# Sums as single steps, a narrower U-product, a first pair in two halves and a new order, in a fused attention and low-rank mixer kernel

## The chip, the cores and the metric

The kernel runs on one NeuronCore of a Trainium2 chip. A core has five engines with instruction queues of their own: TensorE (PE) for matmuls, VectorE (DVE), ScalarE (ACT) and GpSimd (POOL) for elementwise work, and SyncE (SP), which here only issues DMAs. POOL issues most of the loads through a DMA queue of its own, SP the first loads, the transposes by DMA and the stores. Every engine works through its own list in order; semaphores make one wait for another. The metric is the time of one execution on the device in microseconds (us), lower is better.

## The reference

The inputs are q, k, v of 4 batches x 8 heads x 768 tokens x 64, U (768 x 32), V (32 x 768), w_ch1 (512 x 2048) and w_ch2 (2048 x 512), all float32.

```python
scores = scale * np.matmul(q, k.transpose(0, 1, 3, 2))
keep = is_global | is_local          # 8 global keys, 96 local ones, causal
scores = scores + bias[None, :, :, :]            # -slope(head) * distance
scores = np.where(keep, scores, -1000000000.0)
a = np.exp(scores - max); a = a / a.sum()
x = np.matmul(a, v)                  # 4 x 768 x 512, heads side by side
h = x^T @ U @ V                      # rank 32, over the tokens
u = x + h^T
out = u + np.maximum(u @ w_ch1, 0.0) @ w_ch2
```

So: a banded attention, a token mixer of rank 32 with a residual, and an MLP of 512 to 2048 to 512 with a residual.

## The kernel before, in words

The work is cut into 16 pairs of heads (batch b = pair // 4) and, for each batch, an MLP. Every piece of work is a `Task` with a name, an engine and what it depends on (lines 100 to 130). The tasks are put out in an order that is written out by hand, the string `ORDER` (line 23 and on): `Planner.run` (line 135) only checks it against the dependencies and the buffers, and takes the buffer numbers from `SLOTS`. So each engine's list is the order's own, cut to that engine. Attention of the next batch is woven into the MLP of the batch before it.

The names, with p the pair, b the batch:

- `lkp`, `lqp`, `lvp`: loads of K, Q, V (`add_load`, line 345). Pair 0's K and Q come as float32 by SP into scratch memory, and `Ck0.h`, `Cq0.h` cast them to half precision, one head each. All other loads are cast by the DMA, on POOL's queue. `w1_i` and `w2_i` load the weights.
- `TKp`, `TQp`: K and Q are turned, so that the head dimension lies on the partitions (`arrange`, line 531): six 128x128 matmuls with an identity for pairs 0 and 4 to 7, twelve of half width for pairs 1 to 3, a DMA transpose for pairs 8 to 15. `EKp`, `EQp` copy the result from PSUM; pair 0's copy is split in two halves of the tokens. `KOp` is K with the 32 first keys put in front of each block.
- `SBp.s`, `Sp.s`, `EXp.s`, `MKp.s`: bias by matmul (batch 0 alone), scores, exp on ACT, and a multiplication by the mask on DVE (batches 1 to 3). `PVp`: probabilities times V, with a column of ones for the sums; `VCp`, `VGp` prepare V. `RCp`, `NMp`: the division, into `x_sb`; `XCp`: x in half precision.
- `UPp` (`mixed`, line 754): x @ U. For pairs 0 to 7 it also turns x into uT by six identity matmuls (L759); for pairs 8 to 15 `XTp` does that by DMA. The U part (L764) is six 128x128 matmuls per pair whose weights are `uz` (U four times over, so that its 32 columns fill 128) and whose moving operand is x. `TEp` copies the result to `tmp`, `HMp` multiplies it by V, `E0p` and `E1p` bring it to uT.
- MLP-1: u @ w_ch1. Batch 0 does it directly but for one unit (`M1a` to `M1d`, L927 and L951, relus `RL`, `RM`). All else is done by seven products for a 2x2 block of output instead of eight (`ZP1b.z` to `ZP7b.z`, L1024; z is a unit, 0 to 7). They need sums of blocks of w_ch1, `ZSz` (line 998, four DVE instructions of 256 columns for a unit, kept over the batches), and sums of blocks of u, `ZTb` (line 977, four DVE instructions of 768 columns in one task). `ZU`, `ZW`, `ZX` copy partial sums on ACT, `ZA`, `ZB`, `ZD` add and clip on DVE (L1042), `ZR` is a relu on ACT.
- MLP-2, in the same manner: `PAb.g`, `PBb.g` form sums of the hidden layer on DVE (two instructions each, lines 1091 to 1101), `TWa`, `TWb` sums of w_ch2 (line 467), `P1b.t` to `P7b.t` are the products of eight matmuls of 256 columns (`prod`, L1141), `RSb.t` puts the mixer's part in PSUM ahead of them (L1133), `DA` to `DH` add the results to x, `Ob.t` stores.
- `w0` to `w23`: matmuls of zeros that fill PE (L1240).

PE changes between matmuls on 64 rows (`S`, `HM`, `RS` and the half-width turns) and on 128 rows (all others).

Of the kernel before, what the change touches and what calls it, by code (L numbers as in the profile page):

```python
# [21 lines left out]
lk0 ones2 ones3 vz wz iota w6 lq0 ones0 relf w1 lk1 w4 rel3 bias1 bias0 w2 lq1 w0 w3 lk3 mask3 SB0.2 Ck0.0 Ck0.1 vs1  # L22
mask1 TK0 lv0 w7 Cq0.0 EK0.1 SB0.0 w5 mask7 lk2 Cq0.1 bias2 EK0.0 TQ0 lq3 SB0.1 KO0.1 EQ0.1 ones1 EQ0.0 KO0.0 lq2
S0.2 TK1 EX0.2 lv1 S0.1 EK1 TQ1 EX0.1 S0.0 lv2 EQ1 TK3 EX0.0 SB1.0 KO1 u16 SB1.1 bias4 S1.1 VC0 EK3 S1.0 vs0 uz SB1.2
VG0 lv3 EX1.0 KO3 S1.2 TK2 EX1.2 PV0 EK2 EX1.1 lk5 TQ3 RC0 NM0 TQ2 EQ3 SB2.1 KO2 SB2.2 EQ2 SB2.0 VC1 lk4 S2.0 VG1
S2.1 XC0 EX2.0 S2.2 PV1 EX2.2 VC2 lq4 SB3.1 uc EX2.1 RC1 back S3.1 mixl NM1 SB3.2 EX3.1 S3.2 VG2 lq5 SB3.0 VC3 VG3
S3.0 mask0 TK5 EX3.0 PV2 EK5 w1_1 EX3.2 PV3.0 RC2 UP0 RC3.0 w1_7 NM2 XC1 TK4 PV3.1 w1_5 TE0 EK4 PV3.2 XC2 HM0 RC3.1
lv4 RC3.2 UP1 NH3.1 E00 NH3.0 UP2 NM3 w1_3 TE1 UP3.0 TE2 UP3.1 NH3.2 w1_2 KO4 HM1 HM2 E01 TQ5 E02 w1_4 UP3.2 TQ4 TE3
EQ5 lk6 M1a0.3 EQ4 M1c0.3 HM3 S4.1 E13 E03 M1d0.3 EX4.2 lv5 ZT0 M1a0.2 M1c0.2 M1b0.3 EX4.1 w1_0 M1a0.15 RL0.3 M1b0.14
VC4 KO5 M1a0.14 RM0.14 w1_6 vs2 RL0.15 M1d0.2 mask2 S5.0 S4.0 M1b0.2 EX4.0 M1a0.11 EX5.0 MK4.0 M1b0.7 lk7 VG4 RL0.2  # L30
M1a0.7 MK4.2 RM0.7 MK4.1 M1b0.15 RL0.14 ZS3 M1b0.10 RL0.11 mask5 M1b0.6 MK5.0 RL0.7 RM0.15 lq7 ZS7 S5.1 RM0.10
M1b0.11 EX5.2 ZS6 PV4 w2_3 EX5.1 M1a0.10 lq6 RM0.11 M1b0.8 MK5.1 RM0.6 M1a0.8 RC4 RL0.10 NM4 VC5 ZP10.5 w2_1 ZP20.5
RM0.8 ZS5 M1a0.6 ZU0.5 RL0.8 M1a0.1 MK5.2 w2_2 mask6 TK6 M1c0.1 RL0.6 EK6 w2_0 ZP60.5 M1d0.1 TD0 ZW0.5 PA0.3 M1b0.1
lv6 VG5 M1b0.12 PA0.1 ZP50.5 RM0.12 M1b0.4 RL0.1 TK7 ZA0.5 RM0.4 ZP70.5 lq8 PB0.1 PV5 mask4 KO6 M1a0.5 EK7 ZX0.5 RC5
M1a0.4 lk9 NM5 RL0.5 TQ6 RL0.4 TQ7 ZB0.5 KO7 M1a0.12 EQ6 XC5 M1a0.0 EQ7 M1c0.0 lv8 PB0.3 ZP40.5 XC4 ZP30.5 M1d0.0
RL0.12 ZD0.5 M1b0.0 ZR0.5 M1b0.5 RL0.0 PA0.2 S7.0 lv7 RM0.5 UP4 EX7.0 PA0.0 S6.1 TE4 RS0.1 EX6.2 HM4 PB0.2 P20.1 E04
PB0.0 UP5 EX6.1 P10.1 TWa1 lk8 TE5 S6.0 RS0.0 EX6.0 HM5 DA0.1 P20.0 TWa0 lv9 VC6 P30.0 E05 lq10 TWb0 P50.0 VG6 P50.1
TWb1 lq9 P30.1 DF0.0 P60.1 MK6.1 TK8 P10.0 DF0.1 lk10 ZS2 S7.1 VG9 EX7.1 RS0.2 MK6.0 P10.2 DA0.0 EX7.2 MK6.2 P20.2
TQ8 DC0.1 VC7 PV6 MK7.2 VG7 TK9 P60.0 DB0.1 MK7.0 DA0.2 P70.1 RC6 TQ9 DB0.0 MK7.1 P60.2 DD0.1 NM6 PV7 TQ10 P40.1 RC7
XC6 NM7 VC9 lq12 P30.2 DB0.2 XC7 VG8 ZS4 UP6 KO8 UP7 lv11 DG0.1 DF0.2 TE6 P70.0 TE7 ZS1 lk11 HM7 HM6 S8.0 E07 E06  # L40
P50.2 DD0.0 lv14 DC0.0 E17 ZP11.6 KO9 ZT1 ZP11.7 lk12 P70.2 ZU1.7 ZU1.6 ZP21.7 EX8.0 P40.0 lq11 ZA1.7 ZP61.7 DG0.0
S8.1 ZW1.7 MK8.0 VC11 ZP21.6 DD0.2 EX8.2 ZP71.7 ZS0 P40.2 ZX1.7 ZA1.6 EX8.1 ZP11.5 DC0.2 ZP51.7 ZP41.7 ZU1.5 DG0.2
O0.2 ZP61.6 MK8.1 ZR1.7 S9.1 O0.3 ZB1.7 EX9.1 ZP11.4 TK11 ZP61.5 ZP31.7 ZU1.4 MK9.1 ZP21.4 ZW1.5 ZP21.5 O0.1 ZD1.7
EX9.2 ZP61.4 ZP71.5 ZA1.4 ZP21.3 ZA1.5 O0.0 ZX1.5 ZP51.5 ZW1.6 ZP11.3 ZB1.5 ZP51.6 ZW1.4 TK10 ZP71.6 MK9.2 ZU1.3
ZP31.5 ZP71.4 ZA1.3 ZP51.4 ZD1.5 ZX1.4 ZP11.2 VC8 TD1 ZP41.5 ZX1.6 ZB1.4 ZP61.3 VG11 ZP21.2 ZB1.6 ZW1.3 ZP31.4 MK8.2
ZR1.5 ZP31.6 ZP41.4 ZU1.2 ZD1.4 O0.5 ZP71.3 ZR1.4 ZA1.2 ZP61.2 O0.4 ZX1.3 ZP51.3 ZD1.6 TQ12 ZW1.2 S9.0 ZB1.3 ZP11.0
EX9.0 ZP71.2 PA1.2 ZP41.3 ZU1.0 ZP41.6 TQ11 ZX1.2 ZP31.3 MK9.0 ZR1.6 ZP51.2 ZD1.3 PV8 ZR1.3 ZB1.2 TK12 ZP61.0 RC8
ZP11.1 NM8 ZP31.2 lv12 ZU1.1 ZP21.1 ZW1.0 ZP21.0 ZD1.2 XC8 ZP61.1 ZA1.1 ZP51.0 ZP41.2 ZA1.0 ZW1.1 XT8 ZP71.0 PB1.2
ZR1.2 ZP71.1 ZX1.0 UP8 ZP51.1 ZX1.1 ZB1.0 PV9 TE8 KO12 KO10 PA1.3 ZP31.0 ZP41.1 ZP41.0 ZB1.1 lv10 ZR1.1 HM8 ZD1.0
ZR1.0 ZP31.1 RC9 VC12 lk13 RS1.1 ZD1.1 P21.1 KO11 NM9 P11.1 VG12 E08 lq13 S10.1 PA1.0 RS1.0 EX10.2 P11.0 lk14 PA1.1  # L50
EX10.1 P21.0 DA1.0 XC9 S10.0 PB1.3 lq15 S11.0 P51.0 EX10.0 XT9 PB1.0 EX11.0 P51.1 lq14 PB1.1 S11.1 MK11.0 P61.0
EX11.2 DA1.1 lk15 P31.0 EX11.1 DB1.0 MK11.2 P31.1 VC10 MK11.1 UP9 DF1.0 VG10 PV11 MK10.2 TE9 VC14 P61.1 RC11 NM11
lv15 P71.0 DF1.1 XC11 HM9 S12.0 RS1.2 E09 XT11 EX12.0 P11.2 DD1.0 MK10.0 S12.1 TQ14 MK10.1 EX12.1 P21.2 DB1.1 VG14
DC1.0 PV10 TK14 DA1.2 P71.1 RC10 NM10 lv13 P61.2 DD1.1 XC10 UP11 P31.2 EX12.2 TE11 XT10 DC1.1 P41.0 MK12.1 DB1.2 HM11
DF1.2 UP10 P71.2 DG1.0 TE10 KO14 E111 P41.1 MK12.2 VC13 E011 ZP12.6 VG13 DD1.2 S14.0 DG1.1 ZU2.6 HM10 P41.2 EX14.0
E010 O1.0 ZP12.7 ZT2 O1.1 S14.1 ZU2.7 VC15 EX14.1 ZP22.7 P51.2 VG15 EX14.2 ZP22.6 MK14.0 ZP62.6 ZA2.7 ZP52.7 TK15
ZW2.6 ZP62.7 MK12.0 ZP52.6 DC1.2 ZW2.7 ZP72.6 ZP22.4 ZA2.6 ZX2.6 O1.2 ZP72.7 ZP12.4 ZB2.6 TQ15 ZX2.7 ZP42.6 DG1.2
# [106 lines left out]
def kernel(  # L164
# [180 lines left out]
    def add_load(p):  # L345
# [23 lines left out]
        def one(src, dst, g, nm, i):  # L369
            if direct(p, nm):  # L370
                i += 2 * p

                def ldf():
                    nc.sync.dma_start(*by_token(stg32[i], src))
# [527 lines left out]
    def mlp(b):  # L902
# [84 lines left out]
        for z in units:  # L987
# [5 lines left out]
            def sw(i, gs=gs, z=z, a21=a21):  # L993
                if gs is None:
                    return a21 if i == 0 else zs[ZK.index(z)][:, i - 1]
# [296 lines left out]
```

## Time and profile before

| | us |
|---|---|
| median of 3 runs (217.62 to 218.74) | 217.62 |
| the profiled execution | 217.54 |
| its span | 215.8 |
| PE busy | 211.1 |
| DVE busy | 189.3 |
| ACT busy | 138.2 |
| POOL busy | 72.2 |
| first exp starts | 8.11 |
| first MLP matmul starts | 26.85 |
| first product of MLP-2 starts | 54.21 |
| last product of MLP-2 starts | 209.72 |

The span runs from the first to the last instruction of the profiled execution; the time of the execution is 1.7 us longer. Busy means that an instruction of the engine was under way. PE's matmuls overlap, so a busy PE may still be spaced more widely than it could be: the distance from the start of one to the start of the next tells more than the length of one. Times in the text count from the start of the span. The trace gives instructions by line; the names of tasks were put to them by their place in each engine's order.

### The profile page before, as it was taken

The numbers are of one execution on the slowest core, as the hardware profiler recorded it, in microseconds if no ns is written. First come the engines' busy times: TensorE is split into PE (matmuls) and PEld (weight loads), VectorE is DVE, ScalarE is ACT, GpSimd is POOL, SyncE is SP. The second block draws the span as 40 slices with busy tenths as digits, with TensorE's granted clock in tenths as the row PEclk, the third lists the DMA queues.
The fourth block names the chain that finished last, engine by engine and source line by source line (L and its number), as shares of the span: only waits on it lengthen the run. The fifth ranks groups of instructions, "written<-read, shape, count | busy, mean of one in ns | idle before, by whom it ended". The sixth has DMA issues, their size and how long they took to land.

```text
span 215.8 us, 5747 instructions
## 1 busy us (share of the span) xinstructions
PE 211.1 (98%) x2298; PEld 153.7 (71%) x2298; DVE 189.3 (88%) x417; ACT 138.2 (64%) x255; POOL 72.2 (33%) x95
## 2 busy tenths in 40 slices
PE   8998999999999989999999999999999999999996
PEld 3565855676889866566787875667789766668896
DVE  4687977999999998999999899999999975999680
ACT  6999989989924669789886467785722068730000
POOL 8989967873670860013961100000000000000000
DMA  6999999999999999779999957651002310000543
GB/s 166 175 168 156 145 180 177 181 194 196 154 151 157 147 156 159 179 185 127 141 132 129 121 155 144 185 94 36 3 0 51 74 49 3 2 2 3 219 149 122
DMA packets 100731, 26.78 MB, mean 124 GB/s; under 512 B 87744, under 2 KB 98112, under 8 KB 100704
## 3 DMA queue, kind: packets, MB, share of 16 engines
q0 software_dynamic: 71312, 13.34, 80.1%
q1 hardware_dynamic: 29392, 13.07, 28.3%
q8 instruction: 18, 0.29, 0.6%
q14 instruction: 9, 0.07, 0.1%
HBM read 27.56 MB, written 6.29 MB: 157 GB/s over the span
## 4 chain that ended last, share of the span: by engine, by line
PE 91%; ACT 5%; DVE 2%; issue 1%; POOL 0%; POOLq 0%
PE ps L1141 35%; PE ps L1024 26%; PE ps L927 6%; PE ps L652 4%; ACT ep L717 4%; PE ps L1240 3%; PE ps L951 3%; PE ps L764 3%; PE ps L781 2%; PE ps L780 2%; PE ps L521 2%; PE ps L871 2%; PE ps L759 1%; PE ps L1133 1%; PE ps L633 1%
## 5 line engine op out<-in xcount | busy, mean ns | idle before, releaser
L717 ACT ACTIVATE ep<-ps 128x1024 f16<-128x1024 f32 (+1 forms) x48 | 43.9, 957 | 13.3 <-PE ps L652 12.5
L1141 PEld LDWEIGHTS <-htr 128*128 128x128 f16 x392 | 36.3, 98 | 7.3 <-issue 2.3
L265 ACT ACTIVATE zu<-ps 128x384 f32<-128x384 f32 x59 | 27.5, 491 | 8.5 <-PE ps L1024 7.6
L1042 DVE CUSTOM_DVE_ANT_0 htr<-ps,zu 128x384 f16<-128x384 f32 x59 | 31.0, 551 | 1.0 <-PE ps L1024 0.4
L1153 DVE TENSOR_TENSOR x_sb<-x_sb,ps 128x256 f32<-128x256 f32 (+1 forms) x60 | 27.1, 463 | 3.6 <-PE ps L1141 3.1
L1141 PEld LDWEIGHTS <-sA 128*128 128x128 f16 x288 | 27.5, 98 | 3.6
L364 POOL DMA_DIRECT2D vt<-in_v_dram x16 | 16.5, 1032 | 31.7 <-PE ps L781 22.4
L1024 PEld LDWEIGHTS <-w 128*128 128x128 f16 x200 | 18.9, 98 | 11.3 <-issue 0.2
L1141 PE MATMUL ps<-tB,htr 128*128 128x256 f16 (+1 forms) x200 | 24.0, 268 | 0.0
L1141 PE MATMUL ps<-w,sA 128*128 128x256 f16 x192 | 23.6, 273 | 0.0
L1141 PE MATMUL ps<-w,htr 128*128 128x256 f16 x192 | 23.5, 273 | 0.0
L360 POOL DMA_DIRECT2D stgq<-in_q_dram x24 | 19.9, 854 | 10.1 <-DMA qT<-stgq 7.2
L1024 PE MATMUL ps<-uT,w 128*128 128x384 f16 x100 | 23.0, 326 | 0.0
L1024 PE MATMUL ps<-zt,w 128*128 128x384 f16 x100 | 22.6, 326 | 0.0
L360 POOL DMA_DIRECT2D stgk<-in_k_dram x24 | 20.4, 872 | 4.1 <-DMA w<-in_moe_w_ch_dram 2.5
L265 ACT ACTIVATE x<-x_sb 128x768 f16<-128x768 f32 x13 | 10.9, 845 | 10.4 <-DVE x_sb L819 10.3
L730 DVE TENSOR_TENSOR ep<-ep,mask 128x1024 f16<-128x1024 f16 x24 | 16.3, 684 | 0.5 <-ACT ep L717 0.5
L819 DVE TENSOR_TENSOR x_sb<-ps,rcp 128x768 f32<-128x768 f32 x16 | 15.2, 952 | 0.3
L1024 PE MATMUL ps<-zt,zs 128*128 128x384 f16 x64 | 15.3, 326 | 0.0
L927 PE MATMUL ps<-uT,w 128*128 128x384 f16 x80 | 14.7, 326 | 0.0
L652 PE MATMUL ps<-qT,kT 64*128 64x128 f16 x192 | 14.1, 217 | 0.0
L652 PE MATMUL ps<-qT,kO 64*128 64x128 f16 x160 | 12.8, 218 | 1.0 <-DVE htr L1042 0.7
(119 smaller groups left out, 408.6 us busy)
## 6 DMA issues: line engine op xcount, KB each, us to landing
out_dram<-x_sb SPq DMA_DIRECT2D x20, 256.0 KB, 2.4
vt<-in_v_dram POOLq DMA_DIRECT2D x16, 192.0 KB, 7.0
stgk<-in_k_dram POOLq DMA_DIRECT2D x24, 96.0 KB, 6.0
stgq<-in_q_dram POOLq DMA_DIRECT2D x24, 96.0 KB, 5.6
w<-in_moe_w_ch_dram POOLq DMA_DIRECT2D x8, 256.0 KB, 8.6
w<-in_moe_w_ch_dram POOLq DMA_DIRECT2D x4, 512.0 KB, 9.8
out_dram<-x_sb SPq DMA_DIRECT2D x7, 128.0 KB, 2.2
vo<-vt SPq DMA_DIRECT2D x5, 123.8 KB, 2.5
```

The costliest lines, as they stand in the source:

```text
L265: nc.scalar.activation(dst, src, AF.Copy)
L360: nc.gpsimd.dma_start(o[:, i], src[b, h0 + i].rearrange("(n p) d -> p n d", p=P))
L364: nc.gpsimd.dma_start(vt[gv.slot][:, :, :, 0:D], v[b, h0:h0 + 2].rearrange("h (n p) d -> p h n d", p=P),)
L652: nc.tensor.matmul(t[:, hi, j * P:(j + 1) * P], lhs, qt[r, i * P:(i + 1) * P], start=not biased, stop=True, skip_group_check=biased,)
L717: nc.scalar.activation(ep[gep.slot][:, :, lo:512], ps[:, gsc.slot:gsc.slot + 2, lo:512], AF.Exp, scale=qk_scale)
L730: nc.vector.tensor_tensor(ev, ev, mv, ALU.mult)
L819: nc.vector.tensor_tensor(xo, pvo()[:, :, :, 0:D], rcp[p % 2].unsqueeze(3).broadcast_to((P, 2, NB, D)), ALU.mult)
L927: nc.tensor.matmul(ps[:, g.slot, 0:HS], w1[:, dc, jt * P:(jt + 1) * P], ub[:, dc, i * HS:(i + 1) * HS], start=(dc == 0), stop=(dc == NDC - 1),
L1024: nc.tensor.matmul(bank(g), a()[:, i], bq[:, i], start=first and i == 0, stop=last and i == 1, skip_group_check=True,)
L1042: return lambda: nc.vector._custom_dve(TENSOR_ADD_SAT, out=o, in0=x(), in1=y(), s0=3.0e38, s1=0.0)
L1141: nc.tensor.matmul(o if part is None else o[:, part], a[:, j, c0 + cols.start:c0 + cols.stop], bq[:, j] if part is None else bq[:, j, part ...
L1153: nc.vector.tensor_tensor(o, o, x, ALU.add)
```

## The change

Five things are changed at once.

1. The sums of w_ch1 are formed for two units at a time (`ZYay` to `ZYdy`, y = unit // 2): four instructions of 512 columns for two units instead of eight of 256. Each instruction is a task of its own.
2. So are the instructions of `ZT` (`ZTa` to `ZTd`), of the sums of w_ch2 (`TWa` to `TWd`) and of the hidden layer (`PA`, `PB`, `PC`, `PD`). What needs one of these sums now waits for that one, not for all.
3. In pairs 4 to 15 the U part has x as weights and 32 columns of `uz` as the moving operand. Its result stands the other way round, so `XEp` (ACT) copies it to `tmp`, four times over, `XUp` turns it by one 128x128 matmul, and `TEp` copies that.
4. Pair 0's K and Q are loaded in two halves of 64 partitions (four DMAs on SP), cast in four pieces each and turned in two sets of six 64-row matmuls, each with its own PSUM bank.
5. `ORDER`, `SLOTS` and some choices of engine are new. From ACT to DVE go EK3, EQ5, KO4, KO6, KO9, KO10, TE4, TE8, TE9 and XC7; from DVE to ACT KO1, KO15, E01, EQ7, TE11, TE15 and XC15; from SP to ACT KO12, KO13 and the V copies of pair 8; from ACT to SP KO14 and the V copies of pairs 12 and 14. Pair 0's casts and copies are dealt out anew between ACT and DVE.

```diff
-lk0 ones2 ones3 vz wz iota w6 lq0 ones0 relf w1 lk1 w4 rel3 bias1 bias0 w2 lq1 w0 w3 lk3 mask3 SB0.2 Ck0.0 Ck0.1 vs1
+lq0.0 wz iota vz w5 lk0.0 w6 relf lq1 w0 lk0.1 rel3 bias0 bias1 w3 lk1 lq0.1 bias2 w4 bias4 ones0 w1 lk3 w7 Ck0.1 lv0
...
+KO0.0 TQ0.1 uz lq3 KO0.1 EQ0.1 TQ1 lq2 S0.0 EQ1 S0.2 EX0.0 lv1 TK1 S0.1 EX0.2 EK1 SB1.0 u16 TK3 KO1 SB1.2 ones2 EK3
...
-RL0.12 ZD0.5 M1b0.0 ZR0.5 M1b0.5 RL0.0 PA0.2 S7.0 lv7 RM0.5 UP4 EX7.0 PA0.0 S6.1 TE4 RS0.1 EX6.2 HM4 PB0.2 P20.1 E04
-PB0.0 UP5 EX6.1 P10.1 TWa1 lk8 TE5 S6.0 RS0.0 EX6.0 HM5 DA0.1 P20.0 TWa0 lv9 VC6 P30.0 E05 lq10 TWb0 P50.0 VG6 P50.1
+ZP40.5 ZD0.5 UP4 RL0.0 PD0.1 M1b0.5 XE4 PA0.2 ZR0.5 S7.0 PD0.3 RM0.5 XU4 EX7.0 TE4 S6.1 PA0.0 HM4 EX6.1 PC0.2 RS0.0
+P10.0 TWb0 EX6.2 PB0.2 lk8 UP5 TWa1 P20.0 XE5 E04 PC0.0 XU5 TWb1 RS0.1 lq8 TE5 S6.0 HM5 ZYb1 P50.1 E05 PD0.0 DA0.0
...
@@ add_load, pair 0
-                def ldf():
-                    nc.sync.dma_start(*by_token(stg32[i], src))
+                for w in range(2):
+                    rows = slice(64 * w, 64 * w + 64)
+
+                    def ldf(rows=rows, i=i):
+                        d_, s_ = by_token(stg32[i], src)
+                        nc.sync.dma_start(d_[rows], s_[rows])
...
@@ build_t
+            o, x, y = (
+                (tB[:, 1, lo], b22, b12), (b12, b12, b11), (tB[:, 0, lo], b22, b12), (tB[:, 2, lo], b21, tB[:, 0, lo]),
+            )[part]
+            nc.vector.tensor_tensor(o, x, y, ALU.subtract)
...
@@ arrange, pair 0
+                    def turn2(g=g, i=i):
+                        r = slice(64 * i, 64 * i + 64)
+                        for n in range(NB):
+                            nc.tensor.matmul(
+                                ps16[:, g.slot, n * 64:n * 64 + 64],
+                                stg[gs.slot].rearrange("p a b -> p (a b)")[r, n * P:(n + 1) * P],
+                                ident16[r, r], is_transpose=True, start=(n == 0), stop=(n == NB - 1),
+                            )
...
@@ mixed and what follows
+                    if xu:
+                        nc.tensor.matmul(
+                            ps[:, gx.slot, 384:384 + R], xx[:, c], uz[:, c, 0:R],
+                            start=xt and c == 0, stop=(c == NB - 1), skip_group_check=True,
+                        )
+                for c in () if xu else cs:
                     nc.tensor.matmul(
                         ps[:, gx.slot, 384:512], uz[:, c], xx[:, c],
...
+        if xu:
+            def xuevac():
+                copy(ENG[CFG["XE"][p]], tm.rearrange("p (g r) -> p g r", r=R), ps[:, gx.slot, 384:384 + R].unsqueeze(1).broadcast_to((P, P // R, R)))
+
+            def xuturn():
+                nc.tensor.matmul(ps[:, gx.slot + 1, 384:512], tm, ident16, start=xt, stop=True, skip_group_check=True)
+
+            XE = add(ENG[CFG["XE"][p]], 0.28, xuevac, [UP] + xw, name=f"XE{p}")
+            UP = add(PE, 0.06, xuturn, [XE], lat=0.3, name=f"XU{p}")
...
@@ mlp
-            ZT = add(DVE, 2.21, sums_t, dd(range(NDC)) + zt_read, fast=32, name=f"ZT{b}")
+            for n, x, ch, dp in ((0, "a", (0, 1), ()), (2, "c", (0, 1, 2, 3), ()), (1, "b", (2, 3), (0,)), (3, "d", (2, 3), (1,))):
+                ZT[n] = add(DVE, 0.55, sums_t(n), dd(ch) + [ZT[i] for i in dp] + zt_read[n], fast=2, name=f"ZT{x}{b}")
...
-            def sums_s(sw=sw, a11=a11, a12=a12, a21=a21, a22=a22):
-                op = nc.vector.tensor_tensor
-                op(sw(2), a11, a21, ALU.subtract)
-                op(sw(0), a21, a22, ALU.add)
-                op(sw(1), sw(0), a11, ALU.subtract)
-                op(sw(3), a12, sw(1), ALU.subtract)
+                for x, o, i0, i1, op in (
+                    ("a", zy[:, 1], c11, c21, ALU.subtract), ("b", c21, c21, c22, ALU.add),
+                    ("c", zy[:, 0], c21, c11, ALU.subtract), ("d", zy[:, 2], c12, zy[:, 0], ALU.subtract),
+                ):
+                    kept[y].append(add(
+                        DVE, {1: 0.32, 2: 0.43, 4: 0.72}[ng], lambda o=o, i0=i0, i1=i1, op=op: nc.vector.tensor_tensor(o, i0, i1, op),
...
-            P6 = pr(6, gX, lambda sw=sw: sw(1), zt[:, 1], [ZS, ZT, U1], True)
+            P6 = pr(6, gX, lambda sw=sw: sw(1), zt[:, 1], [ZS[2], ZT[1], U1], True)
...
+            for x, o, i0, i1, op, dp in (
+                ("A", s1, a21, a22, ALU.add, r21 + r22 + war(5)), ("C", s2, s1, a11, ALU.subtract, r11 + war(6)),
+                ("B", a21, a11, a21, ALU.subtract, r11 + r21), ("D", s4, a12, s2, ALU.subtract, r12 + war(3)),
+            ):
```

## The prediction

> **What bounds the kernel now.** First the page: busy shares and the 40 slices.
>
> ```profile
> PE 211.1 (98%) x2298; PEld 153.7 (71%) x2298; DVE 189.3 (88%) x417; ACT 138.2 (64%) x255; POOL 72.2 (33%) x95
> DVE  4687977999999998999999899999999975999680
> ACT  6999989989924669789886467785722068730000
> DMA  6999999999999999779999957651002310000543
> ```
>
> TensorE (PE) is busy to the end; ScalarE (ACT) is as full in the first 22 us, and the DMA engines stand at 9 for the first 16 slices (86 us). The waits of PE and a stretch of the chain show how little PE idles later:
>
> ```profile
> PE ps L1240 <- POOL zero L282: 1.0, 1, 1.0
> PE ps L652 <- DVE htr L1042: 0.7, 1, 0.7
> PE ps L521 <- ACT mask L1228: 0.6, 1, 0.6
> PE ps L652 <- DVE x_sb L1153: 0.2, 1, 0.2
> ```
>
> ```profile
> 54.21 0.98 PE ps L1141 x8
> 55.19 0.34 PE ps L759 x6
> 55.53 0.34 PE ps L764 x6
> ```
>
> The first wait is the start, the third the end of the first attention; only 0.7 + 0.2 lie later, at 78.9 and 83.0 us. I added up the start-to-start distances of all blocks in PE's order (a product L1141 0.87 us, a pair of 384-column matmuls 0.325, six turns 0.34, each change between 64-row and 128-row matmuls about 0.22 for both ways): from the first MLP matmul (26.85 us) the real start times follow that sum within 0.3 us for 50 us, lag it by 1.1 us after the two waits, and follow it again to the end. So after 27 us the time is PE's work plus that lag.
>
> Before 22 us ACT sets the pace:
>
> ```profile
> 8.11 2.64 ACT L717 ACTIVATE ep<-ps 128x1024 f16<-128x1024 f32 x3
> 10.62 0.64 ACT L316 ACTIVATE once<-once 128x512 f16<-128x512 f16 x1
> 11.14 0.82 ACT L265 ACTIVATE kT<-ps 128x768 f16<-128x768 f16 x1
> 16.39 3.56 ACT L717 ACTIVATE ep<-ps 128x768 f16<-128x768 f32 x4 [0.49 <-ACT qT L265]
> 19.81 0.54 ACT L1228 ACTIVATE mask<-once 128x384 f16<-128x384 f16 x1
> 21.82 0.89 ACT L265 ACTIVATE x<-x_sb 128x768 f16<-128x768 f32 x1
> ```
>
> And the weights of the second MLP product, from the view of tile w:
>
> ```profile
> L413 POOL DMA_DIRECT2D w<-in_moe_w_ch_dram x4: 740/750/774, 37.1 to 42.0; - x4
> DMA to landing us min/median/max: 5.2/8.9/12.5
> ```
>
> The last part of w2 is issued at 42.04 and lands 12.5 us later, at 54.54; the first product P20.1 starts at 54.21 and the one that needs that part, P10.1, at 55.86. The loads land one behind the other at the pace of the DMA queue.
>
> **The change, part by part.** The sum stands against the profiled execution (217.54 us, span 215.8), 0.08 under the median of 217.62.
>
> *Start.* ACT runs without a pause from the first exp (8.11) to XC1 (21.82) but for 0.49. Of what stands between the exps, the new order moves away bias4 (start to start 0.52), EK3 (0.69, to VectorE) and mask0 (0.41); KO1 comes in (two copies, 0.60 + 0.33, some 0.8 packed). EQ2 now goes ahead of EQ3, and the 0.49 pause can go. That is 1.6 + 0.5 - 0.8 = 1.3 us less. The first exp itself: today it starts 2.6 us after Q lands (5.5), behind two casts, six turns, two evacuations and scores. The new order waits for the fourth half load and then for TQ1, whose data (lq1, now first on POOL's queue) land at about 7 (today lk1, first, lands at 7.16). I get 7.7 instead of 8.11. Two more issues on SP's queue (0.46 each) hold nothing else up, as that queue is empty until 17.9; the four 64-row turns are as many columns as before. E01 moves from VectorE to ACT. Together the first MLP matmul could start 1.4 to 2.3 us sooner.
> But it runs into w2. The new order computes TQ5 (0.33), UP5 (0.51), XU4 (0.06) and P10.0 (0.87) ahead of P20.0, which needs the last part; against the 27.4 us that lie between 26.85 and P20.1 today, and 0.16 less for UP4, that is 29.0 us. From the old start P20.0 would come at 55.9. The same 35 loads stand ahead of and with the last part as now, so I let it land at 54.6, and of the gain 1.2 us are left. Bounds: 0 (the start gains nothing) and -2.3 (the loads land sooner too). I take -1.2, since the landing is the row that both orders share.
>
> *U-product.* In pairs 4 to 15 six matmuls of 128 moving columns become six of 32 and one turn of 128 is added. Six of 128 take 0.34 (above), 56 ns each. The trace has none of 32 columns. The nearest are the 65-column ones (PV), 29 ns apart:
>
> ```profile
> 99.82 0.19 PE L781 MATMUL ps<-vt,ep 128*128 128x65 f16 x1
> 99.85 0.19 PE L780 MATMUL ps<-vo,ep 128*128 128x65 f16 x1
> 99.88 0.19 PE L781 MATMUL ps<-vt,ep 128*128 128x65 f16 x1
> ```
>
> With 29 a pair saves 6 x 27 - 56 = 106 ns. Pairs 4 and 5 lie ahead of the w2 point; the other ten give -1.1 us. Bounds: 14 ns each (a quarter of 56) gives -2.0; no saving at all leaves the added turn, +0.6. I take the row at 29, as the weights loaded are as wide. The Trainium skill ("TensorE: Matmul & The Clock Gate", under "Wait — 56ns, not 53.3ns?") puts the floor at about 25 ns for 32 columns; by it the term would be 10 x (6 x 31 - 56) = -1.3, an estimate, and no run here shows it yet.
>
> *Sums as single steps.* VectorE (DVE) is not the bound, except from 77 to 83.5 us, where PE's 1.1 us are lost: it has ZT1, ZS1 and ZS0 to do, while scores wait for PSUM banks that DVE frees.
>
> ```profile
> 80.83 0.28 DVE L1000 TENSOR_TENSOR once<-w 128x256 f16<-128x256 f16 x1
> 81.15 0.29 DVE L1001 TENSOR_TENSOR w<-w 128x256 f16<-128x256 f16 x1
> 81.47 0.29 DVE L1002 TENSOR_TENSOR once<-w 128x256 f16<-128x256 f16 x1
> ```
>
> A unit's four sums stand 0.32 apart, 1.18 us with the last; eight units take 9.4. The new 16 steps of 512 columns lie between these and the 768-column ones (0.467 apart when independent, 0.586 when the second needs the first); about 0.34 each, 5.4 in all. Only one such step (ZYd1) is left in that stretch in place of eight, and ZP61.7 waits for ZTb1, not for all of ZT1. By my count ZTb1 ends about when PE arrives. I take -1.0 of the 1.1 (bounds -1.1 and 0). PA and PB, TW and ZT keep their instructions, in another order; what DVE gains there (0.12 for each dependent pair pulled apart) is hidden by PE. On balance DVE takes over two KO (0.37 + 0.25 each), one K evacuation (0.69) and two half ones (0.55 each) and gives away E01 (0.96): about +2 us with TE and a cast, covered by the 4 us saved.
>
> *Added waits.* UP, XE (ACT, 0.28 as TE's row), XU, TE, HM: two hops from PE to ACT and back instead of one in 12 pairs. A hop needs about 0.55, as pair 14 shows today: UP's six start distances end at 147.82 (147.48 + 0.34), TE runs from 148.01 to 148.29, HM starts at 148.41, 0.59 later. By my count five hops have 0.55 to 0.59 of other PE work in them (XU4, XU5, XU7 and XU8 to their HM, UP14 to XU14), the rest 0.87 or more. PE waits in order, so everything behind waits too. I take +0.5 in all.
>
> *Fillers.* Four groups of four 128-column zero matmuls stand inside the order instead of three: +0.2. SP trades KO12, KO13 and the V copies of pair 8 for KO14 and those of pairs 12 and 14, POOL's loads change places; hidden by PE, at up to 0.5 if an in-order wait (VC6 for lv6, at about 60) reached PE, which has until 64.
>
> Sum: -1.2 - 1.1 - 1.0 + 0.5 + 0.2 = -2.6, so 214.9 us.
>
> **Rivals.** (1) The start gives nothing (the fourth half load or TQ1's data late): -1.4, 216.1. For it: TQ1 now stands ahead of the first score; against: 1.3 us of ACT work is gone whatever starts first. (2) The loads don't cap: -2.3 instead of -1.2, 213.8; the DMA row of nines speaks against. (3) Half of it: start lost and the DVE stretch stays late, 217.1. (4) Slower: the XE hops are exposed. ACT is in order; if each hop stands behind one more 0.49 us copy or relu, five tight hops cost 0.5 and eight with 0.87 cost 0.17; if four stand behind an exp (1.03) instead, 0.7 to 1.0 each more: 3.9 + 3.5 in place of 0.5, against -3.1 from the rest: 221.8; from 3.1 us of waits on it is no gain, and at 4.2 slower by 0.5%. I put its middle at 219.2. ACT's 64% and the cover counted speak against. (5) DVE bounds the last 20 us: by rows PD3.0 ends 0.3 us ahead of P33.2, with DVE steps 0.467 apart; at 0.586 for all 17 steps in front of it P33.2 would wait 1.7: 216.6. The row speaks against: independent steps do start before the one before ends. The Trainium skill ("VectorE: DVE Perf Modes", "Rules for kernel authors") says the pipe drains between operations whatever one does and that only their count matters; the trace differs, 0.467 against 0.586.
>
> **Chances and range.** Forecast (213.9 to 215.9) 0.45; (1) 0.15; (2) 0.10; (3) 0.13; (4) 0.14; (5) 0.03. A half per cent (1.1 us) is about what a measurement can tell from no change. Faster (below 216.5): the forecast, (2) and most of (1): 0.68; same: (3), (5), the rest of (1): 0.18; slower: (4), 0.14. The range, 213.4 to 218.4, leaves out the fastest of (2) and most of (4); the forecast's own is 213.9 to 215.9.
>
> **What would show it.** XC1 near 20.4; P20.0 right after the last w2 landing, near 54.6; 32-column matmuls 25 to 29 ns apart; no DVE wait of PE near 77 to 83; HM or XU waits on ACT under 0.3 each; last product near 207.1 instead of 209.7. Wrong if PE's waits list names ACT tmp with more than 2 us, or P20.0 comes after 55.5.

## The result, and the profile after

The changed kernel takes 220.25 us (median of 4 runs, 219.77 to 220.94), the kernel before 217.67 us on the same chip: ratio 1.0107, 95% interval 1.0080 to 1.0134. It is 1.1% slower, where 214.9 us was forecast, and outside the range of 213.4 to 218.4. The profiled execution took 220.32 us, with a span of 218.5 us; before it was 215.8, so 2.7 us are to be found. Ranges below hold all runs of a kernel; a run more than 1.5% above the fastest of its kernel is left out of the ratio.

The page of the changed kernel, its busy shares and slices; one digit of a slice stands for 5.5 us:

```profile
PE 211.9 (97%) x2322; PEld 153.1 (70%) x2322; DVE 188.3 (86%) x407; ACT 140.3 (64%) x265; POOL 72.5 (33%) x95
PE   7599999999999999999999899999999999999997
DVE  3458884989999999899999889999999896799781
ACT  5668989899986278998674628979361338840000
PEclk9769999999999999999999999999999999999999
DMA  5999999999999999999999992833000321000154
```

PE's slices in the kernel before:

```profile
PE   8998999999999989999999999999999999999996
```

The shares are those of before. The news is in the first three digits: TensorE (PE) at 5 of 10 in the second slice, its clock at 7 and 6, and ScalarE (ACT), whose first slices read 6999989989 before, at 5668989899. The same stretch as busy time by stages (length, then the time that PE, its weight loads, VectorE, ScalarE and POOL worked in it with the number of instructions, then the granted clock, the share of the DMA engines and GB/s), first two stages of the kernel before, then three of the changed one:

```profile
5.00:10.00 5.00, 4.85 (x73) 2.95 (x71) 2.89 (x8) 4.35 (x9) 4.54 (x7) 1.00 1.54 170
10.00:15.00 5.00, 4.87 (x92) 3.11 (x89) 4.48 (x12) 5.00 (x8) 4.99 (x7) 1.00 1.87 178
```

```profile
5.00:10.00 5.00, 2.05 (x21) 1.13 (x22) 1.79 (x5) 3.19 (x8) 0.66 (x1) 0.82 1.43 204
10.00:15.00 5.00, 5.00 (x56) 2.75 (x56) 3.35 (x7) 2.79 (x6) 3.83 (x8) 0.50 0.96 119
15.00:20.00 5.00, 5.00 (x100) 3.31 (x100) 3.54 (x8) 4.56 (x7) 5.00 (x7) 1.00 2.01 131
```

PE idles three of the five microseconds after 5 us, and does everything from 10 to 15 us at half its clock. Why it idles is in the timeline (start, duration, engine, line, what; in brackets the idle time before it and what ended that):

```profile
5.92 0.94 ACT L268 ACTIVATE stgk<-sA 64x384 f16<-64x384 f32 x2 [2.27 <-DMA sA<-in_k_dram]
6.91 0.35 PE L556 MATMUL ps<-ident,stgk 64*128 64x64 f16 x6 [2.00 <-ACT stgk L268]
7.73 0.36 DVE L270 CAST stgk<-sA 64x384 f16<-64x384 f32 x1 [4.55 <-DMA sA<-in_k_dram]
8.30 0.50 PE L556 MATMUL ps<-ident,stgk 64*128 64x64 f16 x6 [1.04 <-ACT stgk L268]
9.48 0.50 PE L556 MATMUL ps<-ident,stgq 64*128 64x64 f16 x6
10.88 0.50 PE L556 MATMUL ps<-ident,stgq 64*128 64x64 f16 x6
12.64 1.72 ACT L737 ACTIVATE ep<-ps 128x768 f16<-128x768 f32 x2 [0.73 <-PE ps L672]
```

K's halves are waited for until 5.9 and 7.7 us, Q's second half is turned at 10.9 us, and the first exponential runs at 12.64 us instead of 8.11. The six turns of one half take 0.35 us at 6.91 and 0.50 us from 8.30 on: there the clock has fallen. The clock's records say 1.0 until 8.18 us, 0.5 from there to 15.01 us, and 1.0 after.

The list of PE's waits, which named the 0.7 us for DVE's htr before, has lost that and got others:

```profile
PE ps L556 <- ACT stgk L268: 3.0, 2, 2.0
PE ps L1266 <- POOL zero L285: 0.9, 1, 0.9
PE ps L672 <- ACT ep L737: 0.8, 1, 0.8
PE ps L653 <- ACT ep L737: 0.2, 1, 0.2
PE ps L653 <- DVE x_sb L845: 0.2, 1, 0.2
```

The single steps stand apart in the stretch where the sums stood together before (79 to 84 us here), with additions of the product (x_sb) between them:

```profile
81.26 0.41 DVE L1047 TENSOR_TENSOR zs<-w,zs 128x512 f16<-128x512 f16 x1
81.62 0.56 DVE L1019 TENSOR_TENSOR zt<-uT 128x768 f16<-128x768 f16 x1
82.10 0.41 DVE L1179 TENSOR_TENSOR x_sb<-x_sb,ps 128x256 f32<-128x256 f32 x1
82.43 0.55 DVE L1019 TENSOR_TENSOR zt<-uT,zt 128x768 f16<-128x768 f16 x1
```

And the second product's weights, by the view of tile w, are no longer near the front. The last part lands at 56.98 us, and P20.0 starts at 60.53:

```profile
L421 POOL DMA_DIRECT2D w<-in_moe_w_ch_dram x4: 747/787/792, 40.7 to 43.2; - x4
DMA to landing us min/median/max: 5.2/7.0/13.8
```

Where the 2.7 us lie, counted as the prediction did: the start-to-start distances of all blocks in PE's order are summed (32-column matmuls at the 25 ns that the trace now shows), and a block's lag is its start less that sum. "Whole loads" is the second experiment below, here for comparison.

| us | before | after | whole loads |
|---|---|---|---|
| lag at the first MLP matmul | 5.23 | 9.66 | 4.52 |
| lag ahead of DVE's stretch (UP7, 73 to 78 us) | 5.14 | 9.72 | 4.59 |
| lag behind it (ZP51.5, 85 to 90 us) | 6.20 | 9.68 | 4.55 |
| lag behind pair 12's scores (P21.2, 115 to 121 us) | 6.05 | 10.54 | 4.50 |
| lag at the last product (P43.0) | 5.94 | 10.53 | 4.56 |
| work of PE up to there | 203.78 | 202.74 | 202.74 |
| start of the last product | 209.72 | 213.27 | 207.30 |
| from there to the span's end | 6.08 | 5.23 | 5.10 |

Start +4.43, work -1.04, DVE's stretch -1.10, the stretch with a new wait at 120 us +1.01, the end -0.85, the rest +0.25: together +2.7. So the loss is at the start; PE's work and DVE's stretch come out near what was forecast for them.

### The profile page after: what moved, and what is told of

The parts are those of the page before. It is cut to its first block, busy times and chain, and to the rows that moved or that the text cites. A ratio compares the mean times of both kernels' runs of the same rounds, so it can differ in the third digit from the quotient of the medians.

```text
span 218.5 us, 5815 instructions
## 1 busy us (share of the span) xinstructions
PE 211.9 (97%) x2322; PEld 153.1 (70%) x2322; DVE 188.3 (86%) x407; ACT 140.3 (64%) x265; POOL 72.5 (33%) x95
## 3 DMA queue, kind: packets, MB, share of 16 engines
q1 hardware_dynamic: 28672, 13.08, 29.2%
## 4 chain that ended last, share of the span: by engine, by line
PE 74%; DMA 10%; ACT 8%; DVE 3%; issue 2%; POOL 1%; SPq 1%; POOLq 0%; DVEq 0%; ACTq 0%
PE ps L1167 28%; PE ps L1062 23%; PE ps L672 4%; PE ps L967 4%; DMA vt<-in_v_dram 4%; DMA kT<-stgk 3%; DMA sA<-in_k_dram 3%; PE ps L653 2%; ACT ep L737 2%; PE ps L1266 2%; ACT htr L973 2%; PE ps L807 2%; PE ps L908 1%; PE ps L991 1%; PE ps L806 1%
## 5 line engine op out<-in xcount | busy, mean ns | idle before, releaser
L1062 PE MATMUL ps<-zt,zs 128*128 128x384 f16 x76 | 17.4, 326 | 0.0
L1062 PEld LDWEIGHTS <-zs 128*128 128x128 f16 x114 | 11.0, 98 | 7.3
```

What stands on the lines that cost most here:

```text
L1062: nc.tensor.matmul(bank(g), a()[:, i], bq[:, i], start=first and i == 0, stop=last and i == 1, skip_group_check=True,)
```

## The experiments

Theory 1: the half loads land late, because they share the DMA engines with POOL's loads, and a rest of PE behind that halves its clock. The first rival: the new order, with its added steps, is longer as a whole.

The landings, which most of this rests on, as the traces record them (us from the span's start; a and b are the halves; POOL's first load is issued at 1.4 to 1.5 us unless held back, and its first packet is in the last column):

| kernel | K | Q | POOL's first packet |
|---|---|---|---|
| before, whole | 3.85 | 5.50 | 4.11 |
| after (Qa, Ka, Kb, Qb) | 5.90, 7.70 | 3.96, 9.37 | 2.93 |
| before, halves by partitions | 3.85, 6.49 | 7.77, 9.40 | 3.04 |
| the same, POOL held back | 4.00, 4.93 | 5.77, 6.51 | 8.19 |
| before, halves by head | 3.14, 3.64 | 5.99, 7.75 | 3.39 |
| after, POOL held back | 5.44, 6.40 | 4.22, 7.25 | 5.41 |
| after, whole loads (two profiles) | 3.81; 3.75 | 5.28; 6.05 | 4.01; 3.91 |
| the same, memsets first | 3.79 | 4.98 | 4.22 |

**Half loads in the kernel before.** The halves alone, in the other kernel:

```
-                    nc.sync.dma_start(*by_token(stg32[i], src))
+                    d_, s_ = by_token(stg32[i], src)
+                    for w in range(2):
+                        rows = slice(64 * w, 64 * w + 64)
+                        nc.sync.dma_start(d_[rows], s_[rows])
```

> The kernel before with nothing changed but that K and Q of the first pair are each loaded by two DMAs of 64 partitions, K's first; casts and turns wait for both. Theory 'landing': the halves come in one after the other, each taking as long as a whole, so K lands near 5.9 us instead of 3.85 and Q near 9.4 instead of 5.50; the start is 2 to 4 us later and the time is 220 to 222 us. Rival 'the halves land as the whole did' (the same bytes, the same 512 packets): K by 4.1 us, Q by 6.0 us, and 217.7 us (217.4 to 218.2); then it was the order of the changed kernel (Q's half ahead of K's, POOL's loads close behind) that made them late.

222.04 us (221.56 to 222.70), ratio 1.0189 (1.0149 to 1.0229), at the upper end of what theory 'landing' expected. The timelines of SP's queue and VectorE in this kernel:

```profile
0.74 1.43 SPq L376 DMA_DIRECT2D sA<-in_k_dram  x2
2.21 1.26 SPq L376 DMA_DIRECT2D sA<-in_q_dram  x2
...
6.59 0.36 DVE L266 CAST stgk<-sA 128x384 f16<-128x384 f32 x1 [3.25 <-DMA sA<-in_k_dram]
9.49 0.89 DVE L266 CAST stgq<-sA 128x384 f16<-128x384 f32 x2 [2.54 <-DMA sA<-in_q_dram]
```

The first half lands when the whole landed (3.85 us), and every further one is late, though neither casts, turns nor order were touched. With the rest of the kernel as before, these four lines cost 4.3 us: the halves do the harm by themselves, and the new order is not needed for it.

**Whole loads in the changed kernel.** The reverse: casts and turns stay in halves, all else as changed, lk0 and lq0 first in the order.

```
-                for w in range(2):
-                    rows = slice(64 * w, 64 * w + 64)
-                    def ldf(rows=rows, i=i):
-                        d_, s_ = by_token(stg32[i], src)
-                        nc.sync.dma_start(d_[rows], s_[rows])
+                def ldf(i=i):
+                    nc.sync.dma_start(*by_token(stg32[i], src))
...
+                for w in range(2):
+                    rows = slice(64 * w, 64 * w + 64)
```

> The changed kernel with the first pair's K and Q loaded whole again, K first, as two DMAs; casts and turns stay in halves, and all else is as in the changed kernel. Theory 'landing': K lands near 3.9 us and Q near 5.5 us, TensorE's rest before 8.3 us and the low clock go with it, and the 4.4 us by which the start is later than before come back but for some 0.4 us for casts and turns in halves: 216.2 us (215.4 to 217.0), faster than the kernel before. Rival 'the new order': the steps that the new order added (the casts to 16 bits in front of the U-product, the single steps) make the rest of the kernel longer by as much, and the start is made up for later; then the time stays above 219 us whatever K and Q do.

214.48 us (213.71 to 215.64), ratio to before 0.9845 (0.9798 to 0.9891): 5.8 us less than the changed kernel. That is more than theory 1 expected (215.4 to 217.0), and the rival is gone. Busy time by stages:

```profile
5.00:10.00 5.00, 4.50 (x84) 2.63 (x82) 4.42 (x10) 4.53 (x10) 3.63 (x5) 1.00 1.51 169
10.00:15.00 5.00, 5.00 (x100) 3.20 (x95) 3.95 (x9) 4.78 (x8) 5.00 (x9) 1.00 1.93 174
```

84 matmuls in place of 21 from 5 to 10 us, and the clock whole. The lag at the first MLP matmul falls from 9.66 to 4.52 us, and the wait at 120 us isn't there either.

**The clock by itself.** Sixteen more groups of zero products in PE's waits; the halves stay.

```
-    "WV": 8, "WN": 16, ...
+    "WV": 8, "WN": 32, ...
```
In the order w24 to w32 stand ahead of TK0.0, w33 to w36 ahead of TK0.1, w37 ahead of TQ0.0, w38 and w39 ahead of TQ0.1.

> The changed kernel with sixteen more zero products on TensorE in the first 11 us, where it waits for the halves of K and Q; nothing else moves. Theory 'clock': the rest from 4.3 to 8.3 us is what brings the granted clock down to 0.5 from 8.18 to 15.0 us, and of the 4.4 us that the start is late some 1.6 are the 2.3 us of work between 11.1 and 15.0 us that took 3.9. Then the granted clock stays at 1.0 and the time is about 218.6 us (218.2 to 219.2). Rival 'landing alone': TensorE waits for the landings of the halves anyway, the last at 9.37 us, and for ScalarE's chain behind them, so that a faster clock only adds waiting: 220.2 us (219.8 to 220.6), with the first exponential still near 12.6 us.

218.07 us (217.43 to 219.94, 11 runs), ratio to before 1.0006 (0.9988 to 1.0023). The stages again:

```profile
5.00:10.00 5.00, 3.83 (x63) 3.21 (x61) 1.55 (x5) 2.64 (x6) 0.20 (x1) 1.00 1.44 207
10.00:15.00 5.00, 5.00 (x87) 3.15 (x85) 4.14 (x8) 4.15 (x10) 4.10 (x8) 1.00 0.85 118
```

The halves land at least as late as in the changed kernel (K 6.57 and 8.25, Q's last 9.61 us) and the first exponential is still at 12.35 us, but the clock stays at 1.0 and the first MLP matmul starts at 29.89 instead of 31.37 us. That clock is borne out by PE itself: the score matmuls at 12 us stand 0.06 us apart, in the changed kernel 0.11. So half of the 4.4 us was the clock: 2.2 us by the medians, a little more than expected (218.2 to 219.2); the landing alone can't explain it. The profile shows 1.5 of it at that point. It is the slowest of the 11 runs (219.94 us): PE also waits 1.3 us there for VectorE at 100 us, which waits for a store.

**Halves with POOL held back.** Two large memsets ahead of POOL's first load, in the kernel before with halves; one run, for the landings.

```
+            if i == 0:
+                for _ in range(2):
+                    nc.gpsimd.memset(mask, 0.0)
             nc.gpsimd.memset(vt[i][:, :, :, D:DP], 1.0)
```

> The kernel before with K and Q loaded in halves by partitions, and POOL held back by two large memsets ahead of its first load, so that SP's four halves have the DMA engines to themselves; its time says nothing, only the landings count. Theory 'the halves share with POOL's loads': alone they land at about 3.9, 4.7, 5.6 and 6.5 us. Rival 'each half takes as long by itself': 3.9, 6.5, 7.8 and 9.4 us as beside POOL's loads.

4.00, 4.93, 5.77 and 6.51 us: sharing it is. Undisturbed, a half follows the one before by 0.74 to 0.93 us; beside POOL's loads by 1.3 to 2.6 us. Even so the last comes 1.0 us later than the whole did (5.50). The time (222.0 us, one run) says nothing of it, since all loads of POOL are late and something else came up, told at the end.

**The same in the changed kernel.** One memset, half as long.

```
+                if p == 1 and src is q:
+                    nc.gpsimd.memset(mask, 0.0)
                 if p in by_pe:
                     nc.gpsimd.dma_start(*by_token(dst[g.slot], src))
```

> The changed kernel with its half loads left as they are, and POOL held back by one large memset (some 2.6 us) ahead of its first load, so that SP's four halves are nearly through before POOL's packets come. Theory 'sharing': the halves land near 4.0, 4.9, 5.8 and 6.6 us instead of 3.96, 5.90, 7.70 and 9.37, the turn of Q's last half starts near 8 us instead of 10.9, the granted clock stays at 1.0 after 8 us, and the time falls to 216.5 to 218.3 us although the loads of the pairs behind them are 1 to 2.6 us later. Rival 'the halves themselves': landings as in the changed kernel, 219.8 us and more.

218.00 us (217.79 to 218.69, 10 runs), ratio 1.0004 (0.9986 to 1.0022). The last half lands at 7.25 us, 2.1 us sooner, and the time falls by 2.25 us although POOL's first load is issued 2.4 us later and PE waits 1.4 us for VectorE behind the memset. In the profiled run, the slowest of the ten (218.69 us), the clock was at 0.5 from 7.3 to 14.1 us as in the changed kernel, so that part of the expectation did not hold in it; in the nine others the mean clock reads 1.0, which can miss a slow stretch (last section). So how the gain divides between landing and clock is not shown.

**Halves by head.** Are the 64 partitions to blame, or the two DMAs?

```
-                    nc.sync.dma_start(*by_token(stg32[i], src))
+                    d_, s_ = by_token(stg32[i], src)
+                    for h in range(2):
+                        nc.sync.dma_start(d_[:, h], s_[:, h])
```

> The kernel before with K and Q of the first pair each loaded by two DMAs again, but cut by head (all 128 partitions, one head's half of the columns) and not by partitions; the bytes and packets of each DMA are those of the halves by partitions. Theory 'the cut across partitions': with all 128 partitions in each DMA the halves follow one another at the rate of the whole, K complete by 4.2 us and Q by 6.0 us, and the time is that of before, 217.2 to 218.3 us. Rival 'two DMAs instead of one': the second half of K lands some 2.6 us behind its first as in the kernel with halves by partitions (3.85 and 6.49 us), Q's last near 9.4 us, and the time is 221 to 222.5 us.

218.19 us (217.41 to 220.85, 10 runs), ratio 1.0024 (0.9996 to 1.0052): the time is the theory's, the landings fit neither. SP issues these halves in 0.39 to 0.43 us each, not 0.60 to 0.77, and K is complete at 3.64 us, sooner than the whole. Q's halves, requested later, meet POOL's packets (from 3.39 us) and end at 7.75 us instead of 5.50. This fits the reading that what decides is how much of SP's load is through when POOL's begins, and that the cut across partitions loses most as its issues are the slowest; no run varied the length of the issues alone.

**The U-product.** Undone in the changed kernel (the names XE and XU leave the order):

```
-    "XU": (4, 5, 6, 7, 8, 9, 10, 11, 12, 13, 14, 15)
+    "XU": ()
```

> The changed kernel with the U-product of the last twelve pairs as before (128 columns of moving data from 16-bit x, no step that evacuates and no product behind it); halves, single steps and the rest of the order stay. The prediction counted 1.1 us less work on TensorE for it and 0.5 us for the added steps. Theory 'the U-product saves as counted': 220.25 + 1.1 - (0 to 0.5) = 220.8 to 221.4 us. Rival 'the added steps cost what it saves': 219.9 to 220.5 us. Rival 'hops exposed': below 219.8 us.

221.52 us (221.03 to 222.60), ratio to before 1.0170 (1.0126 to 1.0213) against 1.0107 (1.0080 to 1.0134): 1.3 us more by the medians, 0.1 above what was expected; the intervals touch. The profiles bear it out: here the last product starts 0.7 us later than in the changed kernel, though the wait at 120 us (some 0.8) is absent, and 0.3 of the 0.7 lies at the start; that leaves 1.2 us of work. In the changed kernel's timeline six 32-column matmuls take 0.30 us, five distances of 25 ns and the length of the last (0.18):

```profile
102.42 0.30 PE L785 MATMUL ps<-uz,x 128*128 128x32 f16 x6
```

**Single steps put together.** Based on whole loads (214.48 us). In the order, ZYa1 to ZYd1 go to the place of ZYd1, ZTa1 to ZTd1 to that of ZTc1, and ZYa0 to ZYd0 behind ZP71.7.

> The changed kernel with K and Q loaded whole (214.48 us), and twelve of VectorE's single steps put together again between 75 and 82 us as the kernel before had its sums: the four of the sums of the weights for units 2 and 3, the four of the activations' sums of the second image, and the four of the weights for units 0 and 1; nothing else. Theory 'single steps': standing together they keep VectorE from the exponentials' masks and the product's additions for 2 us and more at a time, and TensorE waits 1.0 to 1.3 us as it did in the kernel before at 78.9 and 83.0 us: 215.3 to 216.0 us. Rival 'the order at large': TensorE has other work to do there in the new order and loses under 0.3 us: 214.2 to 214.8 us.

218.31 us (217.49 to 222.24, 12 runs), ratio to before 1.0030 (1.0005 to 1.0055): 3.8 us lost against the 214.48, where 0.8 to 1.5 were expected. A wait of its list and two stages:

```profile
PE ps L1059 <- DVE zt L1016: 1.0, 1, 1.0
```

```profile
80.00:85.00 5.00, 3.38 (x31) 1.88 (x30) 4.90 (x12) 2.52 (x5) 0.45 (x1) 0.87 1.76 133
85.00:90.00 5.00, 5.00 (x39) 2.90 (x38) 4.86 (x13) 3.36 (x6) 0.00 (x0) 0.78 0.78 245
```

In the profiled run PE waits 1.6 of 5 us, and the clock falls behind that as at the start (0.5 from 83.75 to 87.16 us). Its lag rises from 6.57 to 10.25 us across the stretch. (The same profile has a slow start too: Q landed at 6.42 us, and the clock was at 0.5 from 8.65 to 12.07 us.) Six of the other eleven runs have a mean clock of 1.0 and take 217.5 to 218.5 us all the same, so how the 3.8 us divide between waits and clock isn't settled.

**Four of them.** Only ZTa1 to ZTd1, at the place of ZTc1.

> The changed kernel with K and Q loaded whole (214.48 us), and of its single steps only the four of the activations' sums of the second image put together at one place near 77.5 us, as the kernel before had them; the sums of the weights stay apart. Putting twelve steps together cost 3.8 us (218.31 us). Theory 'any four steps in a row hold VectorE too long': the four take 4 x 0.48 = 1.9 us in a row, the mask of the first exponential and the first additions behind them come later by 1.0 to 1.4 us, and TensorE waits about as long: 215.2 to 216.2 us. Rival 'the eight steps of the weights cost it': 214.2 to 214.9 us.

215.73 us (215.00 to 217.71, 8 runs), ratio 0.9905 (0.9871 to 0.9938): 0.85 us over the base beside it (214.88) and within what the theory expected, but the two intervals overlap (0.9838 to 0.9898), so the times alone don't show it. The profile does, at a smaller size: PE waits 0.4 us at 80.2 us for VectorE's htr, and in the two profiles of whole loads its list of waits names none from 76 to 90 us. VectorE has no pause from 68 to 85 us in any of the three, so only the order of its steps differs. So where steps stand matters in that stretch, for four steps by 0.4 us where 1.0 to 1.4 were foreseen.

**The whole third part undone.** Whole loads, two casts each by head, one turn each, as before; the other two parts as changed.

```
-    "C0": "AAADDADD"
+    "C0": "DADDDADA"
```
and the casting and turning code of before in place of that of the halves.

> The changed kernel with the whole of its third part undone: K and Q of the first pair loaded whole, cast in two steps by head over all 128 partitions and turned in one go each, as before; U-product, single steps and the rest of the order as changed. Beside it stands the kernel with whole loads alone (214.48 us), where casts and turns are in halves. Theory 'halves of casts and turns gain nothing': four casts of 64 partitions take about as long each (0.36 and 0.52 us) as two of 128, so that the first exponential comes 0.2 to 0.3 us sooner without them: 214.2 us (213.6 to 214.6). Rival 'the halves shorten the chain from the landing to the first exponential': 214.8 to 215.5 us.

215.34 us (214.99 to 215.62), ratio 0.9885 (0.9862 to 0.9908): in the rival's range, but the interval overlaps that of the kernel with whole loads alone (0.9838 to 0.9898 in its second measurement), so that the halves of casts and turns gain something isn't shown. With Q down at 4.88 us its first exponential runs at 8.86 us; in the kernel below, with casts and turns in halves and Q at 4.98 us, at 8.17 us. It is 0.8 us slower than that one by the medians. PE was at half rate longer in this profile (0.85 us for six turns of 128 columns at 4.71 us, 0.50 at 6.34), so one profile each doesn't part the two effects.

**Memsets first, and whole loads again.** Based on whole loads: ones0 to ones3 moved ahead of lq1 on POOL's queue; beside it the base once more.

> The changed kernel with K and Q loaded whole, and POOL's four small memsets ahead of its first load as the kernel before had them, which holds that load back by some 0.4 us; nothing else. Theory 'sharing': Q's whole load (5.28 us in one profile of the kernel with whole loads, 6.42 in another with the same start) has fewer of POOL's packets beside it and lands by 5.1 us; the time is 214.2 us (213.6 to 214.6). Rival 'POOL's own loads are next': they land 0.4 us later and the score products of the second and third pairs with them: 214.6 to 215.2 us.

> The changed kernel with K and Q loaded whole, a second time beside the two above, on their chip: 214.5 us (214.0 to 215.0) by every theory; it gives the base that the two are compared with.

214.52 us (214.15 to 214.87), ratio 0.9842 (0.9816 to 0.9867), and 214.88 us (214.47 to 215.88), ratio 0.9868 (0.9838 to 0.9898). The memsets held POOL's first load back by only 0.1 us (issued at 1.48 us instead of 1.39), so this is no strong test. The two can't be told apart by these intervals; in its profile the first had Q at 4.98 us, the second at 6.05. Either beats both kernels: 1.3 to 1.6% less than before, and by the medians 2.4 to 2.6% less than the changed one.

## Why the prediction was wrong

**The start** (-1.2; it was +4.4). The step that failed is "two more issues on SP's queue (0.46 each) hold nothing else up", and with it the "7.7 instead of 8.11" for the first exponential, which waits for "the fourth half load". Both took it that four halves move like two wholes. The runs show three things in its place. SP issues a half in 0.60 to 0.77 us, longer than a whole of twice the size (0.45); in the trace of before against that of the changed kernel:

```profile
0.74 0.45 SPq L374 DMA_DIRECT2D sA<-in_k_dram  x1
1.25 0.46 SPq L374 DMA_DIRECT2D sA<-in_q_dram  x1
```

```profile
0.74 0.77 SPq L382 DMA_DIRECT2D sA<-in_q_dram  x1
1.56 1.26 SPq L382 DMA_DIRECT2D sA<-in_k_dram  x2
2.86 0.62 SPq L382 DMA_DIRECT2D sA<-in_q_dram  x1
```

Meanwhile POOL's packets come in between the halves, and the DMA engines are shared for the rest. What the DMA engines moved in the first 8 us, by the DMA view (GB/s in slices of 0.2 us), before and then after:

```profile
GB/s 0 0 0 0 0 0 0 0 0 92 207 215 330 369 369 384 384 384 384 353 292 81 100 96 119 165 154 173 165 131 131 165 188 177 184 184 165 184 181 190
```

```profile
GB/s 0 0 0 0 0 0 0 0 0 0 0 115 253 307 250 119 73 65 92 177 219 227 269 265 231 234 204 238 230 276 215 238 192 219 219 242 250 211 184 230
```

Before, K and Q went through in one piece at up to 384 GB/s. After, one half goes at up to 307, the rate falls to 65 at 3.4 us, and from 4 us it is 180 to 280 for all queues. Third, PE has so little to do while it waits (0.35 us of turns between 4.9 and 8.2 us) that the clock falls, and it crosses the next 6.8 us at half rate; the filler experiment puts that at half of the loss. The other thing that the term counted, 1.3 us less ACT work behind the first exponential, came only in part, as the kernel with whole loads shows: its twelfth exponential starts 12.39 us behind the first (before: 12.80), the first MLP matmul 17.85 us behind the first exponential (before: 18.75). XC1 starts at 21.83 us, not near 20.4.

The Trainium skill ("DMA: Bandwidth & Descriptors", "Rules for kernel authors") says that two transfers to the two halves of the partitions serialise, since both use all 16 DMA engines, and that one transfer of 128 partitions is to be preferred; under "Queues, rings and completion order" it has each engine take turns between the queues. The runs agree (alone 0.74 to 0.93 us apart, beside POOL's loads 1.3 to 2.6). The rule speaks against this part of the change, but it gives no price: alone, the four halves end 1.0 us later than the two wholes did, and POOL's loads add 2.9. The Trainium skill ("TensorE: Matmul & The Clock Gate", "What's actually happening") has the clock go to half after an idle window of 3.4 us, on a window that runs freely. The trace agrees: its records last 3.413 us (before the fall) and 6.827 us (at half). Here the window was not empty: from 4.77 to 8.18 us PE worked some 0.5 us.

**The start's bounds** ("0 (the start gains nothing) and -2.3") left out a loss, and a load that is split and shared can bring one: +4.4 here. Rival (1) named the place, the fourth half load late, and priced it at no more than the gain forgone.

**The cap by w2.** The last part lands at 54.59 us with whole loads, as forecast (54.6), P20.0 follows at 55.40 (29.2 us behind the first MLP matmul, 29.0 counted), and PE's waits don't name it. The start isn't as early there as foreseen: first exponential 8.38 us, and 8.17 with the memsets first (7.7 forecast), first MLP matmul 26.23 and 25.87, so 0.6 and 1.0 us sooner than before in place of 1.4 to 2.3. The gain is smaller than the cap would have left.

**U-product** (-1.1, with +0.2 for fillers): the work up to the last product is 1.04 us less, and undoing the part costs 1.3. The 32-column matmuls are 25 ns apart, not 29 as from the 65-column row; the floor of about 25 ns that the prediction gave from the Trainium skill ("TensorE: Matmul & The Clock Gate", "Wait — 56ns, not 53.3ns?") was the better price for them. That the total still comes out near the forecast is partly luck: without the cap by w2 all twelve pairs count and not ten, and in four of them the added turn takes 0.15 us and not 0.06, where a 64-row matmul follows.

**The added hops** (+0.5): nothing. "ACT tmp" is not among PE's waits, and taking the hops out made nothing faster. Rival (4) is out, and so is (5): among PE's waits the only one for VectorE is 0.2 us long and lies ahead of 25 us.

**Single steps** (-1.0): right in size. The lag rises by 1.06 us across the stretch before and not at all after, with DVE's htr gone from the waits. Both experiments lose by the medians when steps stand together again, and in both PE waits for htr again; the larger one loses more than was at stake. The rest of the order differs in that stretch too, so the 1.1 us aren't shown to be due to the single steps alone.

**What was not in the sum.** At 120 us PE waits 0.8 us for an exponential, since ScalarE waited for a V load (lv10, 8.26 us from issue to landing at 117.93). Its timeline in the changed kernel:

```profile
117.96 1.54 ACT L268 ACTIVATE vo<-vt 128x660 f16<-128x660 f16 x2 [1.22 <-DMA vt<-in_v_dram]
```

In the other profiles of this order that load takes 4.6 to 7.4 us and the wait is absent; what slowed it here stays open. From the last product to the span's end it is 0.85 us less than before; among the profiles of both orders that length runs from 4.8 to 6.1 us, so it isn't put down to the change.

With whole loads the last product starts at 207.30 us, where 207.1 was forecast, and the time is 214.5 to 214.9. That the sum comes out there is partly chance: less at the start, nothing lost on hops, a shorter end.

## What to carry to other kernels

Send a load that the whole kernel waits for as one DMA over all partitions, unless a run shows the split to be faster: here the split cost 4.3 to 5.8 us. If it must be split, look at what other queues load beside it; with POOL held back the last half landed 2.1 us sooner in the changed kernel. When a change moves what PE first waits for, add up how long PE would be without work: here 3.0 us of rest in two pieces were followed by 6.8 us at half rate, and zero products in the gap gave back 2.2 us. Bound every step that splits a transfer on the side of a loss too.

## What else the runs showed of the hardware

POOL's first packet came at 2.93 to 3.39 us where SP's loads were split, and at 3.91 to 4.22 us where they were whole, with POOL's first issue at 1.4 to 1.5 us in all of these. So 2.5 to 2.7 us passed from issue to packet beside whole loads, and 1.5 to 1.9 beside split ones; why isn't shown.

While POOL's memsets ran, VectorE made almost no headway. In the kernel with POOL held back, the rows of POOL and of VectorE:

```profile
1.26 5.39 POOL L330 MEMSET mask<- 128x3072 f16 x2
```

```profile
1.33 2.72 DVE L289 TENSOR_SCALAR once<-once 128x256 f16<-128x256 int32 x1
4.09 2.61 DVE L290 TENSOR_SCALAR ident<-once 128x128 f16<-128x128 f16 x1
```

These operations take 0.29 and 0.20 us in the kernel before. It fits what the Trainium skill says of a port pair that the two lock against each other ("SBUF — State Buffer", "Terms").

The clock column does not tell of every slow stretch: in the profile of the four sums, which was its slowest run, it reads 1.0 throughout, but pairs of score matmuls at 9.2 to 9.6 us stand 0.11 us apart, as at clock 0.5 in the changed kernel, and 0.06 with whole loads. The distances between matmuls are the surer sign. With the same start in the program, two things differ among the four profiles with whole loads. Q landed between 4.90 and 6.42 us, and PE came to its full rate at different times. The run with Q at 4.90 us is the slow one just named: its first exponential runs at 9.68 us, that of the run with Q at 5.28 us, at full rate from 3.8 us on, at 8.38. So the moment of the full rate can outweigh the landing in the scatter of about a microsecond from run to run.
